# A fused attention and gated-MLP kernel: the first batch by halves of the queries, keys copied whole from the fifth pair on, and a new order

## The chip, the cores and the metric

The kernel runs on one core of one Trainium2 chip. The core has five engines that run side by side, each through its own list in order: TensorE (PE, the matrix engine), VectorE (DVE), ScalarE (ACT), GpSimd (POOL) and SyncE (SP, which here only issues transfers). The metric is the time of one execution on the device in microseconds (us). Lower is better.

## What is computed

Attention over 4 batches x 8 heads, 768 positions of 64, then a gated MLP over 4 batches of 768 rows of 512. Attention sees only 6 of the 24 chunks of 32 keys, chosen by an upper bound of the score per chunk:

```
ub = sum(maximum(q * k_min_of_chunk, q * k_max_of_chunk))     # per query and chunk, causal
mask = (chunk of key is among the 6 largest ub) & (key <= query)
attn = softmax(where(mask, q k^T / 8, -1e9));  x = attn v      # heads side by side: 512
h = gelu(x w_in);  u, v = halves of h (512 each)
v_n = (v - mean) / sqrt(var + 1e-6) * g_ln
v_s = w_sg v_n + b_sg                                          # over the 768 positions
out = x + (u * v_s) w_out
```

## The kernel before

**How the work is laid out.** The heads go in 16 pairs; four pairs make a batch. A pair's q, k and v arrive as rows (L519, L528). PE transposes them in groups of three (L536). DVE reduces the keys to minima and maxima per chunk (L564), ACT or DVE copies keys and queries out of PSUM (L441, L444), and POOL casts the queries (L611). PE computes the bounds (`ub`, L646 for pairs 0 to 3, L693 from pair 4 on, two pairs at once), and DVE turns them into a mask: transposes, the largest eight, a comparison, a transpose back (L656 to L673, L702 to L721). Pairs 0 to 3 add the mask to the scores by extra matmuls (L812) with a table IND. From pair 4 on the mask's rows lie in the same operand as the queries (QA), and INDF beside the keys (KA), so that one matmul does both (L765). For that, KA of each head holds 64 rows of keys and 64 of INDF. ACT takes the exponential (L821 and L771), POOL clears what lies above the diagonal (L828, L776), PE multiplies by v (`pv` off the diagonal L844, `pvd` on it L851), and DVE divides by the sums (`rcp` L859, `xs` L861). PE transposes x (`xtr`, L873) and ACT copies it (`xev`, L441).

When a batch's four pairs are done, the MLP follows: the v half of x w_in with gelu (`hv` L889, `gv` L894), its statistics on DVE (`bns` L899), the inverse deviation on POOL (L905), the normalised v (`vhat`, L917), the u half (`hu` L928, `gu` L934), the product with w_sg (`pt`, L946), and on DVE the gating (L963, which adds b_sg, and L967), then w_out (L979), the sum with x (L988) and the store.

**What sets the order.** The building code creates operations one after another and numbers them. Each names what it reads and writes, from which the waits are worked out. The order in which each engine runs its operations is written out by hand in a table, a list of numbers per engine, with a slot for every PSUM tile. Nothing is reordered at run time: an engine, SP too, that waits holds all that stands behind. PSUM has two score slots of 1024 columns and four general slots of 512. Attention times v uses general slots 2 and 3.

**What the change touches.** `scores` (pairs 0 to 3) cuts its 2688 columns per head into pieces of 512, in the order diagonal blocks first; `head` does a whole head; `xtrans` 768 queries at once; `moe_h` splits batch 0's w_in products into three quarters and one quarter of the inner dimension (HSPL). `kside` copies keys in two halves of 64 partitions for pairs 4 to 7 and in one of 128 from pair KSPR = 8 on, where two transfers then move head 1's keys (`kcp`, L577) and put INDF into head 0's operand (`kin`, L580). For pairs 4 to 7, `mask_rows` puts INDF there by a DVE copy (L735) and a transfer (L738). IND's three further copies and INDF are made on DVE (L403, L408). Transfers of k, q and v have three buffers each, so that a load waits for the transposes of the pair three earlier.

Of the kernel before, what the change touches and what calls it, by code (L numbers as in the profile page):

```python
# [6 lines left out]
ALU = mybir.AluOpType  # L7
# [224 lines left out]
def dve(n, over=70, rate=1.0):  # L232
    o = n / rate / 0.96 + over
    return o, o + 83
# [26 lines left out]
def _build(nc, ctx, q, k, v, w_in, g_ln, w_sg, b_sg, w_out, out):  # L261
# [58 lines left out]
    KSPR = 8  # L320
# [5 lines left out]
    HSPL = 1  # L326
    STACT = 1
    INDV = 1
# [69 lines left out]
    for n, (lo, j) in enumerate(((32, 1), (64, 0), (96, 1))):  # L398
        if INDV == 2:
# [5 lines left out]
        else:  # L405
            P.op("act", lambda d, lo=lo, j=j: d.activation(IND[lo:lo + 32, j, :], IND[0:32, 0, :], ACTF.Copy), act(S),
                 ("init", 10 + n), reads=["IND"], writes=[("IND", n)])
    P.op("dve", lambda d: d.tensor_tensor(INDF[:], IND[:, 0], IND[:, 1], op=ALU.add), dve(S, rate=2), ("init", 13),  # L408
         port=True, reads=["IND"] + [("IND", n) for n in range(3)], writes=["INDF"])
# [42 lines left out]
    xT1n = [("xT", 1, dk) for dk in range(NDK)]  # L452
# [133 lines left out]
    def qside(p):  # L586
        s, w, r = p % NQS, p % NW, p % NR
        for hf in range(2):
# [3 lines left out]
            evac("dve" if p in QDVE else "act", lambda hf=hf: qT[r][:, TG * hf:TG * hf + TG],  # L592
# [150 lines left out]

    def scores_full(p):
        w, es = p % NW, p % 2
        pieces = []
        for kb in range(NT):
            pieces.append((128 * kb, 128, kb, 128 * kb))
        for kb in range(NT - 1):
            pieces.append((EOFF[kb], S - 128 * (kb + 1), kb, 128 * (kb + 1)))  # L750
        for i in range(2):
            for c, c0 in enumerate(range(0, ETOT, 1024)):
# [10 lines left out]
                def sc(e, t=t, mms=mms, i=i):  # L763
# [10 lines left out]
                    writes=[("E", es, i, x) for x in range(2 * c, min(2 * c + 2, len(ECUT)))], ps=[t], table="exp")  # L774
# [3 lines left out]
                 ("aff", p, i), reads=[("E", es, i, 0), ("E", es, i, 1)], writes=[("Ed", es, i)])  # L778

    def scores(p):  # L780
        w, es = p % NW, p % 2
        u, ux = SEL[p]
        pieces = []
        for kb in range(NT):
            pieces.append((128 * kb, 128, kb, 128 * kb))
        for kb in range(NT - 1):
            pieces.append((EOFF[kb], S - 128 * (kb + 1), kb, 128 * (kb + 1)))
        cuts = [(0, LO), (LO, 512)] + ECUT[1:] if p < UNM else ECUT
        for c, (c0, c1) in enumerate(cuts):
# [13 lines left out]
            def sc(e, t=t, mms=mms, masks=masks):  # L803
# [20 lines left out]
                writes=[("E", es, i, c if p >= UNM else ("u", 0)[c] if c < 2 else c - 1) for i in range(2)],  # L824
                ps=[t], table="exp")
        for i in range(2):
            ev = E[es][:, i, 0:S].rearrange("p (j x) -> p j x", x=128)
            P.op("pool", lambda g, ev=ev: g.affine_select(ev, ev, pattern=[[0, NT], [1, 128]], compare_op=ALU.is_ge,  # L828
                                                          fill=0.0, base=0, channel_multiplier=-1), gps(S),
                 ("aff", p, i), reads=[("E", es, i, 0), ("E", es, i, 1), ("E", es, i, "u")], writes=[("Ed", es, i)])  # L830
# [366 lines left out]
```

## Time and profile before

| | us |
|---|---|
| median of 3 runs | 218.07 |
| lowest and highest | 216.73, 219.51 |
| the profiled execution | 217.9 |
| its span, first to last instruction | 216.2 |
| PE busy | 206.0 |
| DVE busy | 184.8 |
| ACT busy | 167.8 |
| POOL busy | 88.8 |

The clock granted to PE was full (0.999). A row of a group reads: line, engine, operation, what it writes from what it reads, shapes, count; then the busy time in us and the mean of one in ns; then the engine's idle time before it and what ended that. A row of the chain of work that ended last reads: start, length, engine, target, line, count. A row of the stretches gives the stretch, its length, then busy time and count for PE, PE's weight loads, DVE, ACT and POOL, PE's clock, the DMA share and GB/s. A row of the transfers gives the size of one and the us from issue to landing.

### The profile page before, as it was taken

What the parts mean: (1) busy time and instruction counts of PE and PEld (TensorE: products, weight loads), DVE (VectorE), ACT (ScalarE), POOL (GpSimd) and SP (SyncE); (2) the same over time, 40 slices, a digit from 0 to 9 for tenths busy, and PEclk for the clock granted to TensorE, in tenths of its full rate; (3) what the DMA queues carried; (4) which work ended last, traced back from release to release, by engine and by line L of the source; (5) the groups of instructions that cost most, each with busy time, mean ns of one, the idle gap of its engine ahead of it and who ended that gap; (6) DMA issues with size and microseconds to landing.
All of it is one profiled execution on the core that took longest, in us unless ns stands there. A gap on an engine that the chain in (4) does not pass through costs nothing.

```text
span 216.2 us, 6033 instructions
## 1 busy us (share of the span) xinstructions
PE 206.0 (95%) x2380; PEld 136.2 (63%) x2380; DVE 184.8 (85%) x534; ACT 167.8 (78%) x258; POOL 88.8 (41%) x119
## 2 busy tenths in 40 slices
PE   7989979899989999998999999999999999999994
PEld 3457757655756577775466776879645668645652
DVE  3999998799979999994999798987798776779894
ACT  3378989987689899999769999999977978774000
POOL 8426696981255476633220655565202331002000
PEclk9999999999999999999999999999999999999999
DMA  7999999993999978988999555533101004002108
GB/s 154 219 219 227 250 256 276 320 278 88 229 237 228 215 198 219 235 223 200 229 183 236 121 132 157 143 124 88 41 0 27 3 0 149 3 0 97 49 3 291
DMA packets 84331, 34.31 MB, mean 159 GB/s; under 512 B 77136, under 2 KB 79440, under 8 KB 84304
## 3 DMA queue, kind: packets, MB, share of 16 engines
q1 hardware_dynamic: 84016, 33.54, 66.0%
q8 instruction: 19, 0.31, 0.7%
q10 hardware_dynamic: 288, 0.39, 0.5%
q14 instruction: 8, 0.07, 0.1%
HBM read 24.77 MB, written 6.29 MB: 144 GB/s over the span
## 4 chain that ended last, share of the span: by engine, by line
PE 75%; DVE 15%; ACT 5%; DMA 2%; issue 1%; SPq 0%; DVEq 0%
PE PSG L946 15%; PE PSC L765 11%; PE PSG L979 10%; PE PSG L928 9%; PE PSG L889 8%; PE PSG L536 7%; PE PSG L844 6%; DVE W L564 5%; PE PSG L693 3%; ACT E L771 3%; PE PSG L851 2%; DVE stats L899 2%; DMA kn<-in_k_dram 2%; PE PSG L873 1%; PE PSC L806 1%
## 5 line engine op out<-in xcount | busy, mean ns | idle before, releaser
L771 ACT ACTIVATE E<-PSC 128x1024 bf16<-128x1024 f32 (+1 forms) x72 | 63.2, 931 | 4.9 <-PE PSC L765 4.5
L564 DVE TENSOR_REDUCE W<-PSG 128x12 f32<-128x384 f32 x64 | 32.7, 547 | 7.0 <-PE PSG L536 6.9
L765 PE MATMUL PSC<-QA,KA 128*128 128x128 bf16 (+2 forms) x336 | 37.6, 246 | 0.0
L946 PE MATMUL PSG<-wsgT,vhat 128*128 128x384 bf16 x192 | 34.7, 326 | 0.7 <-DVE uT L967 0.5
L776 POOL TENSOR_SCALAR_AFFINE_SELECT E<-E 128x768 bf16<-128x768 bf16 x24 | 20.7, 862 | 32.9 <-ACT E L771 32.8
L611 POOL CAST QA<-qT 64x768 bf16<-64x768 f32 (+1 forms) x28 | 24.1, 862 | 15.4 <-ACT qT L441 12.8
L765 PEld LDWEIGHTS PSC<-QA,KA 128*128 128x128 bf16 x336 | 24.1, 98 | 8.8 <-ACT E L771 2.5
L946 PEld LDWEIGHTS PSG<-wsgT,vhat 128*128 128x128 bf16 x192 | 17.9, 98 | 12.0 <-DVE uT L967 1.0
L928 PE MATMUL PSG<-xT,winb 128*128 128x384 bf16 x128 | 24.2, 327 | 0.0
L963 DVE SCALAR_TENSOR_TENSOR PSG<-PSG,glnT,bsgbc 128x384 f32<-128x384 f32 x32 | 19.6, 619 | 5.1 <-PE PSG L946 4.9
L979 PE MATMUL PSG<-woutb,uT 128*128 128x512 bf16 (+1 forms) x100 | 23.7, 371 | 0.0
L934 ACT ACTIVATE uT<-PSG 128x384 bf16<-128x384 f32 x32 | 15.6, 490 | 10.0 <-PE PSG L928 9.6
L821 ACT ACTIVATE E<-PSC 128x1024 bf16<-128x1024 f32 (+3 forms) x26 | 21.5, 872 | 2.2 <-PE PSC L812 1.8
L889 PE MATMUL PSG<-winb,xT 128*128 128x512 bf16 x96 | 22.7, 380 | 0.2 <-ACT xT L441 0.2
L441 ACT ACTIVATE KA<-PSG 128x384 bf16<-128x384 f32 (+1 forms) x38 | 18.5, 497 | 5.5 <-DVE W L564 5.4
L844 PE MATMUL PSG<-vx,E 128*128 128x65 bf16 x480 | 19.7, 194 | 1.1 <-DVE XS L861 0.6
L621 POOL CAST vx<-vn 128x768 bf16<-128x768 f32 x16 | 13.4, 841 | 17.6 <-DMA vn<-in_v_dram 15.5
L844 PEld LDWEIGHTS PSG<-vx,E 128*128 128x128 bf16 x480 | 17.5, 98 | 3.1 <-DVE XS L861 0.7
L861 DVE TENSOR_TENSOR XS<-PSG,rden 128x384 bf16<-128x384 f32 x32 | 17.7, 554 | 0.9
L967 DVE TENSOR_TENSOR uT<-PSG,uT 128x384 bf16<-128x384 f32 x32 | 17.6, 554 | 0.7
L905 POOL TENSOR_TENSOR rstd<-rstd,neghalf 128x6 f32<-128x6 f32 x4 | 5.3, 1329 | 31.2 <-DVE rstd L903 31.2
L899 DVE BATCH_NORM_STATS2 stats<-vgb 128x6 f32<-128x512 f32 x24 | 16.1, 687 | 2.0 <-ACT vgb L894 1.6
(87 smaller groups left out, 353.8 us busy)
## 6 DMA issues: line engine op xcount, KB each, us to landing
kn<-in_k_dram SPq DMA_DIRECT2D x32, 192.0 KB, 4.6
qn<-in_q_dram SPq DMA_DIRECT2D x32, 192.0 KB, 4.4
vn<-in_v_dram SPq DMA_DIRECT2D x32, 192.0 KB, 4.6
out_dram<-osb SPq DMA_DIRECT2D x18, 256.0 KB, 2.3
uT<-in_moe_w_sg_dram SPq DMA_DIRECT2D x4, 384.0 KB, 5.6
vgb<-in_moe_w_in_dram SPq DMA_DIRECT2D x3, 512.0 KB, 6.1
KA<-INDF SPq DMA_DIRECT2D x12, 96.0 KB, 3.6
out_dram<-vgb SPq DMA_DIRECT2D x4, 256.0 KB, 2.2
```

The lines of the kernel that those rows point to most:

```text
L564: P.op("dve", lambda d, m=m, op=op, src=src, h0=h0, h1=h1: d.tensor_reduce(W[w][:, m, 12 * h0:12 * h1].rearrange("p (h c) -> p h c", h=h1 ...
L611: P.op("pool", lambda g, i=i, r0=r0, r1=r1: g.tensor_copy(QA[w][i or 0][r0:r1, :], qT[r][r0:r1, :]), gps(S, 250 if i == 1 else 150), ("qca ...
L765: r = e.matmul(t.ap()[:, o:o + n], KA[w][i][:, 128 * kb:128 * kb + 128], QA[w][i][:, q0:q0 + n], start=True, stop=True)
L771: P.op("act", lambda e, t=t, c0=c0, c1=c1, i=i: e.activation(E[es][:, i, c0:c1], t.ap()[:, 0:c1 - c0], ACTF.Exp, scale=SCALE), act(c1 - c0 ...
L776: P.op("pool", lambda g, ev=ev: g.affine_select(ev, ev, pattern=[[0, NT], [1, 128]], compare_op=ALU.is_ge, fill=0.0, base=0, channel_multi ...
L821: P.op("act", lambda e, t=t, c0=c0, c1=c1, n=n: e.activation(E[es][:, :, c0:c1], t.ap().rearrange("p (i x) -> p i x", i=2)[:, :, 0:n], ACT ...
L844: r = e.matmul(t.ap()[:, 65 * qb:65 * qb + 65], E[es][:, i, a:a + 128], vx[w][:, kb, i, :], start=first, stop=False, skip_group_check=True)
L889: r = e.matmul(t.ap()[:, 0:F], xT[s][:, dk, 128 * qt:128 * qt + 128], winb[:, dk, F:DFF], start=(dk == 0), stop=(dk == NDK - 1), skip_grou ...
L899: P.op("dve", lambda d, qt=qt, st=st: d.bn_stats(stats[st][:], vg[qt]), dve(F, 60), ("bns", b, qt), reads=[("vg", qt)], writes=[("stats", ...
L928: r = e.matmul(t.ap()[:, 0:TG], winb[:, dk, 128 * fb:128 * fb + 128], xT[s][:, dk, TG * tg:TG * tg + TG], start=(dk == 0), stop=(dk == NDK ...
L946: r = e.matmul(t.ap()[:, 0:TG], vhat[s][:, sb, 128 * fb:128 * fb + 128], wsgT[:, sb, TG * tg:TG * tg + TG], start=(sb == 0), stop=(sb == N ...
L979: r = e.matmul(t.ap()[:, 0:n1 - n0], gT[s][:, fb, 128 * qt:128 * qt + 128], woutb[:, fb, n0:n1], start=(fb == 0), stop=(fb == NF - 1))
```

## The change

It does these things:

- Pairs 0 to 3 (Q2 = 4): the columns of the scores are laid out by halves of the queries, 768 columns for queries 0 to 383 and 1920 for the rest, with cuts at 512, 768, 1280, 1792, 2304 and 2688. The diagonal is cleared in two operations a head instead of one, and `head` does each half by itself: two tiles, two `rcp`, two `xs`.
- Batch 0: x^T goes by halves of the queries (eight groups and eight copies for four), and the w_in products depend on one half only. The split of the inner dimension is gone (HSPL = 0), and with it these products use general slots 2 and 3 only, as in batches 1 and 2. The gelus of the two halves are marked as two runs.
- KSPR = 4: the keys of pairs 4 to 7 are copied whole, and `kcp` and `kin` transfers take the place of DVE's copy of INDF.
- IND's three copies become transfers on SP (INDV = 3), and INDF is added on POOL (INDP = 1).
- All order lists, the slots and the filler counts are new. There are 1368 operations for 1338: PE 392 for 386, ACT 248 for 252, DVE 414 for 406, POOL 124 for 115, SP 190 for 179.

Read by the operations' numbers, the new lists say this around batch 0. On PE all pv of pairs 0 to 3 and all x^T groups come before the first w_in product, as they did, and three w_sg transposes instead of two. On ACT the 14 gelus of batch 0 come after the last exp of pair 3 and before the first of pair 4. Between its w_in products PE has ten groups of q and k transposes for pairs 6 to 8 where it had four. On POOL three of the four casts of w_in follow pair 3's last diagonal. On SP the load of b_sg, which stood before pair 4's mask rows (`qd`), stands behind them.

```diff
-    KSPR = 8
+    KSPR = 4
...
-    HSPL = 1
+    HSPL = 0
...
-    INDV = 1
+    INDV = 3
+    INDP = 1
+    Q2 = 4
...
+        if INDV == 3:
+            P.op("sp", lambda e, lo=lo, j=j: e.dma_start(IND[lo:lo + 32, j, :], IND[0:32, 0, :]), dmac(), ("init", 10 + n),
...
+    P.op("pool" if INDP else "dve", lambda d: d.tensor_tensor(INDF[:], IND[:, 0], IND[:, 1], op=ALU.add),
...
+    def pieces_of(p):
+        if p >= Q2:
+            return [(128 * kb, 128, kb, 128 * kb) for kb in range(NT)] + \
+                [(EOFF[kb], S - 128 * (kb + 1), kb, 128 * (kb + 1)) for kb in range(NT - 1)]
+        r, a = [], 0
+        for h in range(2):
+            for kb in range(3 * h, 3 * h + 3):
+                r.append((a, 128, kb, 128 * kb))
+                a += 128
+            for kb in range(3 * h + 2):
+                q0 = max(128 * (kb + 1), TG * h)
+                r.append((a, TG * (h + 1) - q0, kb, q0))
+                a += TG * (h + 1) - q0
+        return r
...
-        cuts = [(0, LO), (LO, 512)] + ECUT[1:] if p < UNM else ECUT
+        cuts = [(0, 512), (512, S), (S, 1280), (1280, 1792), (1792, 2304), (2304, ETOT)] if p < Q2 else ECUT
+        if p < UNM:
+            cuts = [(0, LO), (LO, 512)] + cuts[1:]
...
+        for half in range(2) if p < Q2 else (None,):
+            q0, q1 = (0, NT) if half is None else (3 * half, 3 * half + 3)
+            nq, tg = q1 - q0, () if half is None else (half,)
+            off = [(kb, qb) for kb in range(NT) for qb in range(max(kb + 1, q0), q1)]
+            t = ps_g.tile((2, 3))
...
+        for half in range(2) if b == 0 and Q2 else (None,):
+            j0, j1 = (0, NT) if half is None else (3 * half, 3 * half + 3)
...
+            evac(XEV[b] if isinstance(XEV[b], str) else XEV[b][dk], lambda j0=j0, n=n: xT[b % 2][:, dk, 128 * j0:128 * j0 + n],
...
+        if halves:
+            for h_ in range(2):
+                for qt in range(3 * h_, 3 * h_ + 3):
+                    v_part(qt)
+                for fb in range(NF):
+                    u_part(fb, h_)
```

193 lines of the change are left out of this document (102 added, 91 removed), and 118 rows, old and new, of the table TABLE.

## The prediction

> **What bounds the kernel now.** I read the page's engine totals first, then the chain of work that ended last.
>
> ```profile
> PE 206.0 (95%) x2380; PEld 136.2 (63%) x2380; DVE 184.8 (85%) x534; ACT 167.8 (78%) x258; POOL 88.8 (41%) x119
> ```
>
> TensorE (PE) looks full, but a busy PE isn't a PE at its peak. So I cut the span at five marks taken from the timeline and asked for busy times by stretch: 45.70 is the first matmul of batch 0's w_in products, 59.78 its first w_sg product, 99.37 and 114.38 the same two marks of batch 1, and 88.64 the end of a long run of PE pieces in the chain.
>
> ```profile
> core 0: us, PE busy (x) PEld busy (x) DVE busy (x) ACT busy (x) POOL busy (x), PEclk, DMA share, GB/s
> ...
> 4.69:30.00 25.31, 22.90 (x334) 15.34 (x338) 23.99 (x78) 18.91 (x32) 14.23 (x22) 1.00 1.18 234
> 30.00:45.70 15.70, 14.47 (x315) 10.77 (x305) 13.28 (x39) 14.70 (x23) 12.95 (x16) 1.00 1.04 284
> 45.70:59.78 14.08, 14.08 (x106) 8.81 (x104) 13.75 (x48) 10.55 (x19) 5.00 (x7) 1.00 0.75 185
> 59.78:88.64 28.86, 28.31 (x311) 18.95 (x309) 26.88 (x72) 26.21 (x42) 16.17 (x21) 1.00 0.99 218
> 88.64:99.37 10.73, 9.57 (x180) 7.96 (x173) 8.52 (x36) 10.32 (x16) 5.01 (x6) 1.00 0.89 233
> 99.37:114.38 15.01, 14.74 (x117) 8.56 (x117) 13.00 (x44) 11.57 (x23) 4.58 (x5) 1.00 1.07 205
> 114.38:156.00 41.62, 41.62 (x567) 31.42 (x568) 35.86 (x105) 40.41 (x57) 19.93 (x24) 1.00 0.52 129
> ```
>
> The reader is to see that the limit changes. Up to 30 us it is VectorE (DVE): 23.99 of 25.31. From 30 to 45.7 it is ScalarE (ACT): 14.70 of 15.70. From 45.7 to 59.8 DVE is full again (13.75 of 14.08), and the w_sg products wait for its last operation, vhat. From 88.6 to 99.4 ACT is (10.32 of 10.73). Whether PE is at its peak between, I work out from pieces of the chain, each a run of matmuls with nothing between:
>
> ```profile
> 72.27 1.13 PE PSG L693 x32
> ...
> 74.65 0.44 PE PSC L765 x7
> 75.09 0.86 PE PSG L979 x4
> ...
> 77.58 0.65 PE PSG L536 x6
> 78.24 0.88 PE PSC L765 x11
> ...
> 80.64 0.45 PE PSG L844 x15
> ...
> 199.96 7.80 PE PSG L946 x48
> ```
>
> Between the first w_sg product of batch 0 (59.78) and the first w_in product of batch 1 (99.37), PE's order holds 8 w_sg groups of 0.975 (7.80/8: 7.8), 6 w_out groups of 0.86 (5.2), the scores of eight heads at 1.16 (two chunks of 0.44 and one of 640 columns, 0.28) less two chunks done before (8.4), eight heads of attention times v at 0.63 (21 matmuls at 0.45/15: 5.0), two selection groups of 1.13 (2.3), four x^T groups at 0.33 (by columns, from the scores: 1.3) and 17 transposes of q and k at 0.325 (5.5). That is 35.5 us of 39.6. So 4.1 us are lost there, and most of it where ACT is full. A shorter ACT list there, and a shorter DVE list before 59.78, are what can pay.
>
> **The change part by part.** I numbered the operations as the code creates them, and read the old and new order lists by these numbers. Unit costs, from the groups by line:
>
> ```profile
> L403 DVE COPY IND<-IND 32x768 bf16<-32x768 bf16 x3 | 1.1, 351 | 0.1
> ...
> L408 DVE TENSOR_TENSOR INDF<-IND 128x768 bf16<-128x768 bf16 x1 | 0.5, 547 | 0.0
> ...
> L735 DVE COPY KA<-INDF 64x768 bf16<-64x768 bf16 x4 | 2.6, 656 | 0.1
> ...
> L859 DVE RECIPROCAL rden<-PSG 128x6 f32<-128x6 f32 x32 | 6.1, 191 | 5.1 <-PE PSG L851 4.5
> L861 DVE TENSOR_TENSOR XS<-PSG,rden 128x384 bf16<-128x384 f32 x32 | 17.7, 554 | 0.9
> L988 DVE TENSOR_TENSOR osb<-PSG,XS 128x512 f32<-128x512 f32 x18 | 12.1, 681 | 1.5 <-PE PSG L979 1.4
> L564 DVE TENSOR_REDUCE W<-PSG 128x12 f32<-128x384 f32 x64 | 32.7, 547 | 7.0 <-PE PSG L536 6.9
> L441 ACT ACTIVATE KA<-PSG 128x384 bf16<-128x384 f32 (+1 forms) x38 | 18.5, 497 | 5.5 <-DVE W L564 5.4
> L441 ACT ACTIVATE xT<-PSG 128x768 bf16<-128x768 bf16 x16 | 13.1, 824 | 1.7 <-PE PSG L873 1.6
> L611 POOL CAST QA<-qT 64x768 bf16<-64x768 f32 (+1 forms) x28 | 24.1, 862 | 15.4 <-ACT qT L441 12.8 <-PE PSC L765 1.6
> L602 ACT ACTIVATE rT<-qT 128x576 f32<-128x576 f32 x12 | 8.3, 689 | 0.1
> L894 ACT ACT_TABLE_LOAD x4 | 5.1, 1283 | 0.1
> ```
>
> DVE loses three IND copies (3 x 0.351), INDF (0.547) and the four KA copies of pairs 4 to 7 (4 x 0.656): 4.2 us. The halves give it eight more reciprocals (8 x 0.191) and turn eight multiplications of 384 columns into sixteen of 192. From 384 to 512 columns costs 0.127, so a column is 1 ns, and 192 columns take 0.36: 16 x 0.36 less 8 x 0.554 is 1.3. Together 2.9 us come back; DVE's net is -1.3.
>
> ACT loses eight key evacuations (pairs 4 to 7 whole: 4 per pair become 2), 8 x 0.497 = 4.0 us, and gets eight x^T copies of 384 columns for four of 768: 8 x 0.497 less 4 x 0.824, +0.7. The gelu that now may run in two bursts doesn't in this order: all 14 gelus of batch 0 stand between the last exp of pair 3 and the first of pair 4, with only copies and relus among them. In the old order such copies stand in the same run, and the row shows four table loads for four batches. So I cost this at nothing.
>
> The Trainium skill, page "ScalarE: Activation LUTs", section "Table sets: the hidden batching unit", asks that calls be batched by table set, and says that cheap functions like copy are in every set. A real second run would be against that rule, at two loads; by this order the rule gives no extra load either, and the sum is the same.
>
> PE has the same matmuls, in more groups. POOL gets INDF. No addition of this width is on POOL in the trace: a POOL cast of as many columns takes 0.862, two passes 1.7; either way it runs among POOL's first operations and is first read after pair 4's keys, so I take nothing. The IND copies become three small DMAs (48 KB) behind eight loads. The eight transfers of KA (96 KB each) stand in series between a pair's keys and its scores. The nearest transfers:
>
> ```profile
> KA<-INDF SPq DMA_DIRECT2D x12, 96.0 KB, 3.6
> ...
> QA<-Dt SPq DMA_DIRECT2D x24, 36.0 KB, 1.9
> ...
> bsgbc<-in_moe_b_sg_dram SPq DMA_DIRECT2D x1, 384.0 KB, 6.3
> ```
>
> IND lands within 1.9 to 3.6 us; the masked scores that read it wait for eight reductions (8 x 0.547) and a selection anyway: nothing. KA takes two transfers in turn, 7.2 at 3.6 each. Pair 4's keys are read out before pair 3's last exp, and in the new order the scores that need both transfers come five w_sg groups after the first: hidden. Without that cover each pair would cost up to 7.2.
>
> INDF on POOL has a second price. DVE's subtraction of 24 columns should cost a fraction of an operation of 384 (0.554). Beside a POOL cast it took this:
>
> ```profile
> 27.65 0.82 POOL L437 CAST vhat<-uT 128x768 bf16<-128x768 f32 x1
> 27.73 0.78 DVE L583 TENSOR_TENSOR W<-W 128x24 f32<-128x24 f32 x1
> ```
>
> The Trainium skill, page "SBUF — State Buffer", section "SBUF: two separate sides", says that DVE with two SBUF inputs and GpSimd lock each other out for a whole instruction; the trace agrees. By the rows a meeting costs at most 0.6, and four copies of 0.656 that could meet POOL leave DVE; I take 0.
>
> Now the path. Call T the end of pair 3's last exp (41.1).
>
> ```profile
> 40.68 0.41 ACT L821 ACTIVATE E<-PSC 128x256 bf16<-128x256 f32 x1
> ...
> 45.52 1.00 DVE L702 STREAM_TRANSPOSE U<-PSG 128x288 f32<-128x288 f32 x2
> 45.70 4.26 PE L889 MATMUL PSG<-winb,xT 128*128 128x512 bf16 x19
> ...
> 46.72 1.28 ACT L894 ACT_TABLE_LOAD   x1
> ...
> 56.89 2.82 DVE L917 TENSOR_SCALAR vhat<-vgb,mv,rstd 128x512 bf16<-128x512 f32 x6
> ```
>
> Step 1, T. DVE drops 2.3 us ahead of pair 2's masks (IND, INDF, one KA copy), but the new order puts minima and maxima of pair 4 and three half-heads there, so pair 3's masks come where they came. ACT has as many operations up to T as before. I take -0.5 (bounds -1.5 and +1).
>
> Step 2, to the first w_sg product. After T, PE runs two half-heads (0.63 each with the multiplications hidden behind the next), then x^T halves that wait for ACT's copies, then pair 4's selection: DVE starts its transposes at T+3.8, where it now does at T+4.4. The w_in products wait for the last of POOL's w_in casts, three of which now follow pair 3's diagonal masks, with a query cast among them (three of 1024 columns at 1.1, by the columns of the 0.862 row, and 0.862: 4.2): about T+4.2, against T+4.6. From the transposes on DVE has the 14.2 us of before (45.52 to vhat's end), less one w_sg evacuation moved ahead (0.5), plus six reductions of pairs 6 and 7 moved in (6 x 0.547): 17.0. So the w_sg products start at 40.6 + 3.8 + 17.0 = 61.4, 1.6 later than 59.78. But PE has by then done six more transposes of q and k (6 x 0.325) less 0.16 of scores: 1.8. Net -0.2.
>
> Step 3, to batch 1's w_in products. ACT's list there loses five copies and one relu, 5 x 0.497 + 0.689 = 3.2, and DVE's six reductions are done. PE's work is 34.7 by the same sum (14 transposes, 0.16 more of scores). Of 4.1 us lost I let 2.1 remain: 36.8, so 98.2, against 99.37. The bounds are 0 and 4.1 regained; I take the middle, since PE, now 35 of 37, becomes the limit.
>
> Step 4, batch 1's w_in products: the 15.0 of before, less two transposes, with 0.16 more of scores: 14.5, so 112.7, against 114.38, with 0.5 more work done ahead (a transpose and 0.16). After that the work is the same and PE is full (41.62 of 41.62 in the next stretch), so 1.7 + 0.5 = 2.2 us stay to the end: 217.9 - 2.2 = **215.7**. The profiled execution (217.9) stands 0.2 under the median of the three runs, 218.07, so I make no correction.
>
> Step 5, SP. It is a queue in order, and eleven issues are added.
>
> ```profile
> 45.19 2.15 SPq L433 DMA_DIRECT2D bsgbc<-in_moe_b_sg_dram  x1
> 50.76 1.86 SPq L726 DMA_DIRECT2D QA<-Dt  x3
> ```
>
> The broadcast of b_sg (bsgbc) is issued at 45.19, ahead of pair 4's masks, which held SP until 50.76. In the new order it stands behind them, ten issues later. At 0.62 an issue (1.86/3) that is 56.2 with masks at 50, landing at 62.5 with its 6.3; the first product that adds b_sg comes at 61.4 + 0.975, 62.4. I cost it at 0, since two more w_sg groups fit before PE has no free slot; it has no margin.
>
> **The rivals.** *More is gained.* If T comes 1.5 earlier and the ACT-bound stretch gives all 4.1 back, it is 215.7 - 1.0 - 2.1 = 212.6. For: ACT is full in that stretch, and 3.2 us leave its list. Against: DVE is full in step 2. *Nothing is gained.* The reductions moved ahead of vhat make PE idle, and PE takes ACT's place without regaining: step 3 returns 0.8 instead of 2.0 and T comes 0.5 late instead of early: 215.7 + 1.2 + 1.0 = 217.9, as now. For: 13.75 of 14.08 on DVE. *Slower: b_sg comes late.* Its place is SP behind pair 4's masks. PE has slots for two w_sg groups and then stops; past 64 each microsecond is one on the path. It makes the kernel slower than before from 2.2 later than that, 66.2. [...]
>
> **How the numbers follow.** The forecast has 0.50, more gained 0.19, nothing gained 0.20, slower 0.11. The forecast's own range is 214.2 to 217.0. The range leaves out a part of the first rival (0.07) and the last one's upper half and a little more (0.08): 211.8 to 220.8. About 2% (4.4 us) is what a measurement of this kernel can tell from no change: faster than 213.7 is the first rival and a little of the forecast's edge, 0.21; over 222.4 only the late b_sg with more behind it, 0.09; within 2%, 0.70.
>
> **What would show it.** Step 1: the exp that ends pair 3 near 40.6. Step 2: the first w_sg matmul near 61.4, released by DVE's vhat, with one gelu table load per batch. Step 3: ACT's share in the stretch before batch 1's gelu falls, and the first w_in matmul of batch 1 comes near 98. Step 4: the first w_sg matmul of batch 1 near 112.7. Step 5: no wait of the b_sg product for a DMA. Wrong would be: more than one gelu run per batch, PE waiting for keys of pairs 4 to 7 or for w_out, T later than 42, or a time lost after batch 1, where I see no change of work.

## The result, and the profile after

The changed kernel takes 219.75 us (median of 19 runs, 218.06 to 220.96), the kernel before on the same chip 218.93 (19 runs): ratio 1.0053, 95% interval 1.0030 to 1.0075. The forecast was 215.7: 4.05 us under the measured time, and a gain of 1% where a loss of 0.5% was measured. The stated range, 211.8 to 220.8, holds the time. The direction is wrong. The profiled execution has a span of 217.6, where the kernel before had 216.2.

Two stretches of the changed kernel, one ahead of the end of pair 3's last exp (T), one from the first w_sg product of batch 0 to the first w_in product of batch 1, and the page's totals (columns as in the table of stretches above):

```profile
PE 204.9 (94%) x2397; PEld 137.5 (63%) x2412; DVE 182.4 (84%) x542; ACT 163.9 (75%) x254; POOL 91.7 (42%) x128
```

```profile
30.00:42.67 12.67, 12.21 (x274) 9.82 (x272) 10.89 (x43) 12.64 (x20) 11.17 (x19) 1.00 1.04 291
63.81:101.75 37.94, 35.66 (x472) 26.70 (x477) 34.97 (x107) 32.46 (x49) 20.64 (x26) 1.00 0.98 224
```

And the same second stretch in a second profile of the kernel before, which was taken as an experiment below:

```profile
60.48:100.41 39.93, 37.86 (x483) 26.91 (x481) 35.38 (x108) 36.52 (x57) 21.28 (x27) 1.00 0.92 220
```

The savings in work are real: ACT is 3.9 us shorter over the span (163.9 against 167.8; 3.3 by the forecast's sum), and DVE 2.4 (182.4 against 184.8; 1.3 by the sum). That ACT has 4.1 us less in the second stretch (32.46 against 36.52) is another matter: of the eight key and query copies that are fewer there, one is saved by whole keys, and the new order has moved seven to stages ahead of it (`a_none` below). From 30 us to T ACT has no gap left, 12.64 of 12.67. The marks of the forecast, from the timelines of TensorE and ScalarE of the changed kernel:

```profile
47.68 0.82 PE L948 MATMUL PSG<-xT,winb 128*128 128x384 bf16 x4 [0.20 <-DVE U L708]
...
63.81 2.12 PE L1000 MATMUL PSG<-wsgT,vhat 128*128 128x384 bf16 x12
...
101.75 1.67 PE L929 MATMUL PSG<-winb,xT 128*128 128x512 bf16 x7 [0.78 <-ACT xT L447]
...
115.67 2.11 PE L1000 MATMUL PSG<-wsgT,vhat 128*128 128x384 bf16 x12
```

```profile
40.94 1.73 ACT L841 ACTIVATE E<-PSC 128x1024 bf16<-128x1024 f32 x2
...
48.24 1.28 ACT L954 ACT_TABLE_LOAD   x1
```

Beside the forecast's marks stand those of both profiles of the kernel before. They show how far marks move from one execution to the next: about 1 us by the end.

| mark, us | before | before, second profile | forecast | after |
|---|---|---|---|---|
| T | 41.09 | 41.64 | 40.6 | 42.67 |
| first w_in product, batch 0 | 45.70 | 46.04 | 44.8 | 47.68 |
| first w_sg product, batch 0 | 59.78 | 60.48 | 61.4 | 63.81 |
| first w_in product, batch 1 | 99.37 | 100.41 | 98.2 | 101.75 |
| first w_sg product, batch 1 | 114.38 | 115.47 | 112.7 | 115.67 |
| span | 216.2 | 217.2 | 214.0 | 217.6 |

The start is late from T on. The stage from the first w_sg product to batch 1's first w_in product is shorter (37.94 against 39.59 and 39.93), but the stage ahead of it is longer by more (21.14 from T, against 18.69 and 18.84): from T to batch 1's first w_in product the changed kernel takes 59.1 us, the kernel before 58.3 and 58.8. What follows the last mark is as long as it was (101.9 us, 101.8 before).

The masks of pairs 1, 2 and 3 (last step of each, VectorE's timeline), in the changed kernel and in the second profile of the kernel before:

```profile
19.82 0.48 DVE L679 STREAM_TRANSPOSE Dt<-Dn 128x288 bf16<-128x288 bf16 x1
...
28.54 0.43 DVE L679 STREAM_TRANSPOSE Dt<-Dn 128x288 bf16<-128x288 bf16 x1
...
35.38 0.47 DVE L679 STREAM_TRANSPOSE Dt<-Dn 128x288 bf16<-128x288 bf16 x1
```

```profile
19.77 0.47 DVE L673 STREAM_TRANSPOSE Dt<-Dn 128x288 bf16<-128x288 bf16 x1
...
26.74 0.48 DVE L673 STREAM_TRANSPOSE Dt<-Dn 128x288 bf16<-128x288 bf16 x1
...
33.88 0.48 DVE L673 STREAM_TRANSPOSE Dt<-Dn 128x288 bf16<-128x288 bf16 x1
```

Pair 1's mask comes at the same time; pair 2's comes 1.75 us later (28.97 against 27.22). The first theory was that such late masks starve ScalarE and so make T late. The second theory was that VectorE's whole list ahead of T is the bound, the third that transfers landing late take back any lead, the fourth that T hangs on a chain round several engines.

### The profile page after: what moved, and what is told of

Same layout as the page of the kernel before. It is cut to its first block, busy times and chain, and to the rows that moved or that the text cites. A ratio compares the mean times of both kernels' runs of the same rounds, so it can differ in the third digit from the quotient of the medians.

```text
span 217.6 us, 6124 instructions
## 1 busy us (share of the span) xinstructions
PE 204.9 (94%) x2397; PEld 137.5 (63%) x2412; DVE 182.4 (84%) x542; ACT 163.9 (75%) x254; POOL 91.7 (42%) x128
## 4 chain that ended last, share of the span: by engine, by line
PE 71%; DVE 18%; ACT 5%; DMA 2%; issue 2%; POOL 1%; SPq 0%; DVEq 0%
PE PSG L1000 13%; PE PSC L787 10%; PE PSG L948 8%; PE PSG L929 8%; PE PSG L1033 8%; PE PSG L542 6%; DVE W L570 6%; PE PSG L871 5%; PE PSG L699 3%; PE PSG L905 2%; PE PSG L877 2%; DMA kn<-in_k_dram 2%; DVE W L589 1%; PE PSC L826 1%; DVE vhat L982 1%
## 5 line engine op out<-in xcount | busy, mean ns | idle before, releaser
L798 POOL TENSOR_SCALAR_AFFINE_SELECT E<-E 128x768 bf16<-128x768 bf16 x24 | 21.1, 878 | 31.0 <-ACT E L793 30.7
L841 ACT ACTIVATE E<-PSC 128x1024 bf16<-128x1024 f32 (+4 forms) x26 | 21.3, 865 | 2.1 <-PE PSC L832 2.1
L929 PE MATMUL PSG<-winb,xT 128*128 128x512 bf16 x92 | 21.8, 379 | 1.1 <-ACT xT L447 0.8
L1033 PE MATMUL PSG<-woutb,uT 128*128 128x512 bf16 (+1 forms) x89 | 21.5, 369 | 0.6
L871 PE MATMUL PSG<-vx,E 128*128 128x65 bf16 x480 | 21.1, 194 | 0.9 <-DVE XS L889 0.8
L889 DVE TENSOR_TENSOR XS<-PSG,rden 128x384 bf16<-128x384 f32 (+1 forms) x40 | 18.9, 474 | 1.1
L447 ACT ACTIVATE qT<-PSG 128x384 f32<-128x384 f32 x28 | 13.3, 496 | 8.0 <-PE PSG L542 8.0
L447 ACT ACTIVATE KA<-PSG 128x384 bf16<-128x384 f32 x30 | 15.1, 512 | 4.0 <-DVE W L570 3.8
L934 ACT ACTIVATE vgb<-PSG 128x512 f32<-128x512 f32 x24 | 14.0, 597 | 5.3 <-PE PSG L929 5.3
```

The lines of the kernel that those rows point to most:

```text
L447: P.op("act", lambda e: e.activation(dst(), src(), ACTF.Copy), act(n), tag, reads=reads, writes=writes, ps=ps, shift=shift)
L841: P.op("act", lambda e, t=t, c0=c0, c1=c1, n=n: e.activation(E[es][:, :, c0:c1], t.ap().rearrange("p (i x) -> p i x", i=2)[:, :, 0:n], ACT ...
L871: r = e.matmul(t.ap()[:, 65 * (qb - q0):65 * (qb - q0) + 65], E[es][:, i, at[kb, qb]:at[kb, qb] + 128], vx[w][:, kb, i, :], start=x == 0, ...
L929: r = e.matmul(t.ap()[:, 0:F], xT[s][:, dk, 128 * qt:128 * qt + 128], winb[:, dk, F:DFF], start=(dk == 0), stop=(dk == NDK - 1), skip_grou ...
L1033: r = e.matmul(t.ap()[:, 0:n1 - n0], gT[s][:, fb, 128 * qt:128 * qt + 128], woutb[:, fb, n0:n1], start=(fb == 0), stop=(fb == NF - 1))
```

## Experiments: which part does it

All ratios are to the kernel before on the same chip. First each part was undone alone.

**IND back on VectorE** (`a_ind`).

```diff
-    INDV = 3
-    INDP = 1
+    INDV = 1
+    INDP = 0
```

> The changed kernel with IND's three copies and INDF back on DVE, at the places of the old order; all else as changed. Theory 1 (the new startup order makes the masks of pairs 2 and 3 late, its parts are innocent): DVE gets 1.6 us of work back ahead of pair 2's masks, so the last exp of pair 3 moves later by 0.5 to 1.6 and the time rises by 0.3 to 1.5 over the changed kernel, to about 1.007 to 1.012 of the kernel before. Rival 2 (the three small transfers hold up the loads behind them on SP): the time falls by 0.5 to 1.2, to the kernel before or under it.

Measured 219.61, ratio 1.0047 (1.0015 to 1.0078): as the changed kernel. T came at 42.07, but batch 1's first w_in product at 101.75 again. IND's transfers and INDF on GpSimd are neutral in time, as the prediction had them; neither move expected for this run came.

**Keys of pairs 4 to 7 in halves again** (`a_k8`).

```diff
-    KSPR = 4
+    KSPR = 8
```

> The changed kernel with the keys of pairs 4 to 7 evacuated by halves again (KSPR = 8): eight more ACT copies, four DVE copies of INDF, eight transfers fewer. Theory 1: whole keys are what gives 1 to 2.5 us back between the first w_sg product of batch 0 and that of batch 1, so without them the time rises by 1 to 2.5 over the changed kernel, to 1.010 to 1.017 of the kernel before. Rival (the transfers hold up SP and the loads behind them): the time falls by up to 1.

221.56, ratio 1.0141 (1.0092 to 1.0189), T at 44.47: whole keys gain 1.9 us in this order. They gain it ahead of T, where ScalarE has four more key copies here. From the first w_sg product to batch 1's first w_in product this run takes 37.61 us (66.26 to 103.87), no more than the changed kernel.

**Batch 0 by whole queries again** (`a_q0`), each whole operation where its second half stood.

```diff
-    Q2 = 4
+    Q2 = 0
```

> The changed kernel with pairs 0 to 3 and x^T of batch 0 whole again, each at the place where its second half stood. Rival 3 (the halves' extra DVE operations, 2.9 us, are what costs): the time falls by 1 to 2 under the changed kernel, below the kernel before. Theory 1: the order remains, and the first halves that filled PE are gone: between -0.5 and +1 of the changed kernel.

222.45, ratio 1.0187 (1.0142 to 1.0233), T at 44.35: the halves gain 2.8 us in this order. With whole queries ScalarE stands idle 1.12 us ahead of an exp at 32.00 and 1.27 at 39.00; with halves it has no gap there.

**The new order alone** (`a_none`): all three undone. What is left of the change are the new lists and slots, and HSPL = 0.

```diff
-    KSPR = 4
+    KSPR = 8
-    INDV = 3
-    INDP = 1
-    Q2 = 4
+    INDV = 1
+    INDP = 0
+    Q2 = 0
```

> The new order alone: the changed kernel with keys of the first eight pairs in halves by ScalarE and VectorE as before, batch 0 by whole queries, IND on VectorE; only the order of the lists is the new one. If the parts add up (keys whole were worth 1.9 us and the halves 2.8 us in this order, IND nothing): 4.7 us above the changed kernel, ratio to the kernel before 1.025 to 1.029. If both parts relieve the same stretch of VectorE ahead of T (theory 2): less than the sum, ratio 1.018 to 1.023.

224.36, ratio 1.0270 (1.0231 to 1.0309). The parts add up: 4.7 us above the changed kernel. T came at 45.24, and the first w_sg product at 68.6. So the new order by itself costs 5.9 us, 3.6 of them ahead of T against the second profile, and the parts bring back 4.7. The stage behind the first w_sg product is nearly as short as in the changed kernel, with ScalarE busy 33.61 us instead of 36.52:

```profile
68.60:106.89 38.29, 36.06 (x475) 26.61 (x478) 33.88 (x107) 33.61 (x50) 20.49 (x26) 1.00 0.84 208
```

So it is the order that took the work out of this stage, and it put it ahead: from T to the first w_sg product this run takes 23.4 us.

**Whole keys alone in the old order** (`b_k4`), the transfers put on SP where the changed kernel has them.

```diff
-    KSPR = 8
+    KSPR = 4
```

> The kernel before with one part of the change alone: keys of pairs 4 to 7 whole, with the two transfers a pair put on SP ahead of pair 4's mask rows and, for pairs 6 and 7, behind the loads of pairs 10 and 11. Theory 1: 4 us leave ACT's list and 2.6 DVE's with the startup order unharmed, so 1 to 2 us are gained: 0.991 to 0.996 of the kernel before. Rival (the transfers cost as much as they save): 0.998 or more.

221.39, ratio 1.0116 (1.0060 to 1.0171). T is 40.79 and the first w_in product comes at 44.97, 0.7 earlier than in the first profile of before, but behind it TensorE waits for a whole key's copy and for a head's PSUM tile, and the stage behind the first w_sg product takes 42.3 us (60.32 to 102.61):

```profile
67.12 0.55 PE L542 MATMUL PSG<-identF,kn 128*128 128x128 f32 x3 [1.00 <-ACT KA L447]
...
89.27 0.62 PE L871 MATMUL PSG<-vx,E 128*128 128x65 bf16 x15 [1.26 <-DVE osb L1042]
```

**Halves alone in the old order** (`b_q2`).

```diff
+    Q2 = 4
```

> The kernel before with one part of the change: batch 0's attention, x^T and w_in products by halves of the queries, in the order of before as far as halves allow (their places, and those of a few neighbours ahead of 60 us, chosen anew); keys, IND and the loads as before. If halves gain by themselves what they are worth in the new order (2.8 us): ratio to the kernel before 0.986 to 0.992. Rival (halves only give back what the new order takes from the startup; in the old order the first w_in product waits for the same last head, and VectorE has eight more pairs of reciprocal and product): 0.998 to 1.006.

225.74, ratio 1.0331 (1.0292 to 1.0369). This doesn't price the halves: the places chosen anew also moved the start, and the first mask came at 16.30 instead of 13.5 to 14.1. And all six executions were granted 0.992 of TensorE's clock (0.94 from 30 to 60 us in the profile). Inconclusive. That a part of the change costs time in the other order rests on `b_k4` alone.

**The kernel before once more** (`b_same`), for the spread.

> The kernel before once more, unchanged, for a second profile of it: how far do the marks move from one execution to the next? In its first profile the last exp of pair 3 ended at 41.09 and the first pair's mask was there at 13.49; every profile of the new order, and of the old order with whole keys, has that first mask at 13.6 to 14.6. If the 0.5 us belong to the execution (landing of the first k rows), this profile has the first mask at 13.6 to 14.5 and T later by as much; if they belong to the kernels, 13.4 to 13.6 and T at 41.0 to 41.2.

T at 41.64, the first mask at 14.10, span 217.2. So 0.55 of the 1.58 us by which T seemed late belong to the execution. T is late by 1.0. Counted from the first mask of the same profile T is at 27.6 and 27.5 in the kernel before and at 28.7 in the changed one (42.67 less 13.95), which says nearly the same.

## Experiments: why T is late

**Pair 3's mask early** (`a_d3`), VectorE's list only (`dn` and `dt` are the mask's last two steps; `kmm` are reductions of keys, `wev` copies of w_sg, `rcp` and `xs` the two steps of a half-head):

```diff
-  m8.3 xs.0.0.1 kmm.5.0.0 kmm.5.0.1 wev.1 dn.3 rcp.0.1.1 xs.0.1.1 wev.0 kmm.5.1.1 rcp.1.0.0 xs.1.0.0 dt.3
+  m8.3 dn.3 dt.3 xs.0.0.1 kmm.5.0.0 kmm.5.0.1 wev.1 rcp.0.1.1 xs.0.1.1 wev.0 kmm.5.1.1 rcp.1.0.0 xs.1.0.0
```

> The changed kernel, with one edit in the order of VectorE: the last two steps of pair 3's mask (the difference and its transpose) go up to right behind its MAX8, ahead of pair 0's and pair 1's half heads, the sums of pair 5 and two w_sg copies, so that the mask should be there near 32 us where the changed kernel had it at 35.85. Theory 1 (masks behind other VectorE work starve ScalarE, and that is what made the end T of pair 3's last exp late): T falls from 42.67 to 41.7 to 42.2, ratio to the kernel before 1.000 to 1.003. Theory 2 (VectorE's whole list ahead of T is the bound, and a mask that goes forward only pushes the half heads and sums back): T the same or up to 1 us later, ratio 1.005 to 1.010.

220.26, ratio 1.0089 (1.0051 to 1.0127). The mask is there 4.15 us earlier, at 31.70, and T doesn't follow. VectorE and ScalarE of this run:

```profile
31.22 0.48 DVE L679 STREAM_TRANSPOSE Dt<-Dn 128x288 bf16<-128x288 bf16 x1
```

```profile
41.14 1.73 ACT L841 ACTIVATE E<-PSC 128x1024 bf16<-128x1024 f32 x2
```

T is 42.87. The run has a gain and a loss of its own: pair 2's mask came 0.49 earlier, and ScalarE waits 0.80 at 32.91 for a reduction of pair 5, which the edit pushed back. But in the changed kernel ScalarE has no gap from 28 us to T, so nothing there waits for pair 3's mask; theory 1 falls for this mask.

**Less work on VectorE** (`a_sum`). Pairs 4 and 5 take their chunks' minima and maxima from 8 of 32 rows.

```diff
-                    src(0, 128).rearrange("p h (c x) -> p h c x", x=32), axis=AX.X, op=op),
+                    src(0, 128).rearrange("p h (c x) -> p h c x", x=32)[:, :, :, 0:32 if p not in (4, 5) else 8], axis=AX.X, op=op),
```

> The changed kernel with the block minima and maxima of the keys of pairs 4 and 5 taken over 8 of the 32 rows of a block (so those two pairs select by fewer rows): eight reductions of 0.5 us become some 0.15 us, about 3 us less on VectorE between 25 and 38 us, where it has no idle stretch in the changed kernel. Theory 2 (VectorE's whole list ahead of T is the bound): T falls from 42.67 to 40.5 to 41.7, ratio to the kernel before 0.998 to 1.002. Theory 4 (T hangs on a chain that goes round VectorE, TensorE and ScalarE: pair 2's late queries, its scores, the exps that free the tiles; spare time on VectorE only turns into waits): T at 42.2 to 42.9, ratio 1.003 to 1.007.

220.03, ratio 1.0053 (1.0017 to 1.0088), T at 42.75. The time taken out turns into waits on VectorE:

```profile
26.46 0.48 DVE L662 STREAM_TRANSPOSE U<-PSG 128x288 f32<-128x288 f32 x1 [0.69 <-PE PSG L652]
32.36 0.56 DVE L450 COPY wsgT<-PSG 128x768 bf16<-128x768 bf16 x1 [0.91 <-PE PSG L493]
```

Theory 2 falls: VectorE's total isn't the bound. The first row is pair 2's mask, waiting for its bounds on TensorE. ScalarE still has no gap from 28.0 to T.

**Pair 2's queries loaded earlier** (`a_q2`). In the changed kernel TensorE stops here:

```profile
18.81 0.88 PE L542 MATMUL PSG<-identF,kn 128*128 128x128 f32 x6
20.41 0.52 PE L542 MATMUL PSG<-identF,qn 128*128 128x128 f32 x3 [0.72 <-DVE Dt L679]
```

The row names VectorE, whose pair 1 mask ended at 20.30, but these transposes read head 1's queries of pair 2, a load that SP issued at 14.92 and that took 5.4 us here. One issue was moved on SP (the text on record calls these rows the last quarter):

```diff
-  kn.3.0 kn.3.1 vn.0.0 qn.2.1
+  qn.2.1 kn.3.0 kn.3.1 vn.0.0
```

> The changed kernel with one issue moved on SP: the last quarter of pair 2's q rows goes ahead of pair 3's k rows and of the first v rows, so that it is issued at 12.6 us or so instead of 14.92. Single late load: TensorE's wait at 20.41 (0.72) goes, pair 2's mask comes 0.5 to 0.7 earlier than 28.97, T at 42.0 to 42.3, ratio to the kernel before 1.002 to 1.005. Theory 4 (a chain round several engines): the wait goes and another takes its place; T within 0.3 of 42.67, ratio 1.004 to 1.007.

219.74, ratio 1.0052 (1.0022 to 1.0082). TensorE's wait at 20.41 is gone, so it was the load; pair 2's bounds start at 24.64 instead of 25.05, its mask comes at 28.57 instead of 28.97, and T at 42.25 instead of 42.67: 0.41, 0.40 and 0.42.

What carries this to T is not the mask. ScalarE's last wait ahead of T ends at 27.95 in the changed kernel, a microsecond before that mask, and from there to T it has no gap:

```profile
27.95 0.87 ACT L447 ACTIVATE qT<-PSG 128x384 f32<-128x384 f32 x2 [0.75 <-PE PSG L542]
```

These copies wait for pair 4's queries from TensorE, and those transposes stand in its list right behind the bounds of pairs 2 and 3. So the chain of work that ended last goes:

```profile
25.05 2.38 PE PSG L652 x35
27.95 0.88 ACT qT L447 x2
```

From the end of that wait to T lie 14.7 us in all seven profiles with this list of ScalarE and no later wait (the changed kernel, `a_ind`, `a_ind_kn`, `a_v1`, `a_sum`, `a_q2`, `a_lead`: 14.71 or 14.72). From pair 2's mask to T they have 13.4 to 13.7. In `a_d3` the wait ended at 27.47, and 14.6 and the 0.80 make its T. The kernel before had another limit: its last wait ended later, with less of the list behind it.

```profile
31.06 1.44 ACT L441 ACTIVATE KA<-PSG 64x384 bf16<-64x384 f32 x3 [0.94 <-DVE W L564]
```

That is its second profile; T follows 10.6 later. Up to T ScalarE is busy 30.7 us in the changed kernel and 30.9 in this profile. So T is late by waits alone. Pair 2's bounds start at 25.05 where they started at 23.18, 1.87 later. The late load made 0.4 of it. Where the rest comes from isn't isolated, nor what it costs that pair 3's bounds now stand ahead of pair 4's queries (they were at 30.16): no run moved these alone. One piece is to be seen in the changed kernel, VectorE's subtraction for pair 2, which these bounds wait for, and the one for pair 3:

```profile
24.20 0.80 DVE L589 TENSOR_TENSOR W<-W 128x24 f32<-128x24 f32 x1
...
25.65 0.17 DVE L589 TENSOR_TENSOR W<-W 128x24 f32<-128x24 f32 x1
```

The first takes 0.80 for 24 columns, beside a cast on GpSimd from 23.87 to 24.96, as such a subtraction did before; the second takes 0.17.

Four runs tried other places for many operations at once, chosen with a simple model of the lists. A piece of VectorE's list in `a_place` shows the kind:

```diff
-  dt.0 kmm.2.1.0 kmm.2.1.1 kmm.2.0.1 kmm.2.0.0 rel.1 kev.2.1 qev.3.1 qev.3.0 rel.3 utr.1 m8.1 dn.1 dt.1
+  dt.0 rel.1 kmm.2.0.1 kmm.2.1.0 kmm.2.1.1 qev.3.1 kev.2.1 kev.2.0 kmm.2.0.0 utr.1 m8.1 dn.1 qev.3.0 dt.1
```

> The changed kernel with IND and INDF on VectorE as before and the places of instructions and PSUM tiles ahead of 120 us chosen anew on all five engines (whole keys, halves, one gelu run stay): TensorE keeps 342 of 392 places in sequence, VectorE 331 of 418, ScalarE 207 of 248. Pair 1's bounds and mask go ahead of pair 3's query copies, pair 2's queries and sums come earlier on VectorE, loads of k stand ahead of key copies on SP. Theory 4 (places, not work, make T late): T 1 us or more ahead of 42.67, ratio to the kernel before 0.994 to 1.000. Rival (whatever the places, landings and the full VectorE take a lead back by 102 us): T earlier, ratio 1.002 to 1.006.

> The changed kernel, all its parts as they are, with places over the whole kernel chosen anew but the startup nearly left alone (T expected within 0.4 us of 42.67); loads of k ahead of key copies on SP, evacuations and reductions of the stage from 60 to 100 us in another sequence. If the stage behind the startup holds time that places can give back: first w_in product of batch 1 at 100.8 or earlier, ratio 0.996 to 1.001. Rival (landings pace that stage, and vary from execution to execution): ratio 1.003 to 1.006.

Five of the six executions of `a_place` were granted 0.991 or 0.992 of the clock and aren't compared (median 225.94, no ratio); the sixth, at 0.999, took 221.52; `a_place2` took 227.29, ratio 1.0378 (1.0330 to 1.0426). In both the first mask came late (15.63 and 20.25 against 13.95): what was moved ahead of 14 us spoilt the start. So the next two left that part alone.

> The changed kernel with IND and INDF on VectorE and the places of instructions and PSUM tiles between 14.5 and 120 us chosen anew on all engines; what runs ahead of 14.5 us is left as it is. If places make T late and the stage behind it long: pair 1's to 3's masks earlier, T at 41.6 to 42.2, first w_in product of batch 1 at 100.5 or earlier, ratio to the kernel before 0.996 to 1.001. Rival (what is moved earlier is given back at landings, at PSUM tiles, or at the lock between VectorE and GpSimd): T at 42.3 or later, or earlier without gain at 102 us, ratio 1.003 to 1.010.

> The changed kernel with all its parts, places between 14.5 and 120 us chosen anew for the end of the kernel only: T is to stay where it is (42.4 to 42.9), and the stage from the first w_sg product to the first w_in product of batch 1 is to shrink from 37.94 by 0.9 (loads of k ahead of key copies, other sequences of evacuations). If places hold time there: first w_in product of batch 1 at 100.9 or earlier, ratio 0.998 to 1.002. Rival: the stage stays 37.6 or longer, ratio 1.003 to 1.010.

220.68, ratio 1.0109 (1.0071 to 1.0148), and 221.00, ratio 1.0128 (1.0083 to 1.0174). T was 43.25 and 43.53, and pair 2's mask 29.23 and 30.26. The stage behind the first w_sg product did shrink, to 37.1 and 37.3 from 37.94, but the first w_sg product came 1.3 and 0.9 later. They show no better order. Of theory 4 the chain above is shown: VectorE, TensorE's bounds, ScalarE.

## Experiments: why a lead doesn't last

`a_ind` had T 0.60 earlier than the changed kernel, `a_q2` 0.42; neither ended earlier. A timeline of TensorE for each, in this sequence:

```profile
92.70 0.55 PE L542 MATMUL PSG<-identF,kn 128*128 128x128 f32 x3 [0.84 <-DMA kn<-in_k_dram]
```

```profile
93.51 0.55 PE L542 MATMUL PSG<-identF,kn 128*128 128x128 f32 x3 [1.13 <-DMA kn<-in_k_dram]
```

The same k load is waited for: head 1's rows of pair 10, which SP issues behind pair 8's key copy, a step that itself waits for an evacuation.

**That load ahead of the key copy, with IND on VectorE** (`a_ind_kn`).

```diff
-  kn.10.0 kcp.8 kn.10.1
+  kn.10.0 kn.10.1 kcp.8
```

> The changed kernel with IND and INDF made on VectorE as before (that run had its first w_sg product 0.64 us earlier than the changed kernel, 63.17 against 63.81, yet its first w_in product of batch 1 at the same 101.75, and in it TensorE waits 0.84 us for a k load at 92.70), and one edit more on SP: the second half of pair 10's k load is issued ahead of the key copy of pair 8, which waits for its evacuation. Theory 3 (the lead is lost to this load, which the key copy holds back on SP): the wait at 92.70 goes, the first w_in product of batch 1 comes near 101.1, ratio to the kernel before 1.001 to 1.003. Rival (the lead would be lost anyway, to VectorE or ScalarE in the same stage): wait gone or smaller, but w_in at 101.6 to 101.8, ratio 1.004 to 1.006.

219.36, ratio 1.0050 (1.0021 to 1.0080). The k wait is gone, but neither expected mark came: T was 42.65 (its first mask 0.6 later than the changed kernel's), and batch 1's first w_in product 103.06. In this execution b_sg landed late for VectorE, and w_out later for GpSimd (a wait of 3.28 at 73.34, where the changed kernel has 1.59):

```profile
64.90 0.62 DVE L1017 SCALAR_TENSOR_TENSOR PSG<-PSG,glnT,bsgbc 128x384 f32<-128x384 f32 x1 [0.77 <-DMA bsgbc<-in_moe_b_sg_dram]
```

`a_d3` waits 0.52 at the same place. So b_sg, which the new order issues at 59.65, has no margin.

**A sixth of the v traffic of pairs 4 to 15**, in both kernels (`a_v1`, `b_v1`); the rest of v is left out.

```diff
-                vn[s][:, :, i, :], bass.AP(v.tensor, (2 * p + i) * S * DH,
-                                           [[DH, 128], [128 * DH, NT], [1, DH]])), dmac(),
+                vn[s][:, 0:(NT if p < 4 else 1), i, :], bass.AP(v.tensor, (2 * p + i) * S * DH,
+                                           [[DH, 128], [128 * DH, NT if p < 4 else 1], [1, DH]])), dmac(),
```

> The changed kernel with less to load: of the 24 v loads of pairs 4 to 15 only the first 128 rows of each head are moved (one sixth of 192 KB), the rest of the tile keeps older rows; every instruction stays. The DMA engines are 90 to 99% busy up to about 65 us in both kernels, and three runs of the new order whose first w_sg product came 0.4 to 0.9 us earlier had lost that lead by 102 us, each at another load (a k load, b_sg, w_out). Theory 3, widened (from 45 to 100 us the new order is paced by landings, so that a lead is given back to whichever load is late): with a sixth of the v traffic the first w_in product of batch 1 comes 0.8 us or more earlier than 101.75, ratio to the kernel before 0.995 to 1.001. Rival (VectorE, 27.6 of 28.9 us busy between 59.78 and 88.64, paces it): first w_in product at 101.4 or later, ratio 1.003 to 1.006.

> The same cut of the v loads (pairs 4 to 15, one sixth of each moved) in the kernel before, to set beside the changed kernel with that cut. Theory 3: the old order has slack against its loads (no wait for a DMA of more than 0.2 us was seen on TensorE or VectorE from 45 to 100 us), so nothing much moves: ratio 0.997 to 1.000, and the cut kernel of the new order comes down to it or below. Rival: both unchanged, the pair as far apart as the uncut ones.

`a_v1` 219.21, ratio 1.0033 (1.0010 to 1.0056); `b_v1` 218.65, ratio 0.9991 (0.9962 to 1.0020). The stretch from the first w_sg product to batch 1's first w_in product, in `a_v1`:

```profile
64.27:101.09 36.82, 35.98 (x478) 26.39 (x475) 33.62 (x107) 32.53 (x49) 20.75 (x26) 1.00 0.75 188
```

With the DMA share down from 0.98 to 0.75 the stage takes 36.82 instead of 37.94; in the old order the same cut changes nothing (60.68 to 100.28, 39.6). But the stage ahead took 22.0 us from T instead of 21.1, so from T to batch 1's first w_in product only 0.3 us are left (58.8 against 59.1). In time it is worth 0.2%, inside the two intervals. That part of the stage is paced by landings is possible, and not shown by this.

**Three issues moved on SP** (`a_lead`): pair 2's queries as in `a_q2`, that k load as in `a_ind_kn`, and b_sg ahead of pair 4's mask rows, where SP stood idle.

```diff
-  kn.3.0 kn.3.1 vn.0.0 qn.2.1
+  qn.2.1 kn.3.0 kn.3.1 vn.0.0
...
-  ws.2 qd.4.1
+  ws.2 wb qd.4.1
...
-  kn.10.0 kcp.8 kn.10.1
+  kn.10.0 kn.10.1 kcp.8
```

> The changed kernel with three issues moved on SP and nothing else: the last quarter of pair 2's q rows ahead of pair 3's k rows (T was 42.25 with it), b_sg ahead of pair 4's mask rows, where SP stands idle from 49.8 to 52.7, and pair 10's second k quarter ahead of pair 8's key copy. Theory 3 (a lead is lost at these two landings): no wait for b_sg nor for the k load, first w_in product of batch 1 at 101.3 or earlier, ratio to the kernel before 1.001 to 1.004. Rival (another landing or engine takes it: w_out's, the stores', VectorE): first w_in product at 101.6 or later, ratio 1.004 to 1.007.

218.89 against 218.70, ratio 1.0012 (0.9983 to 1.0041): level with the kernel before. SP's and TensorE's timelines:

```profile
49.85 0.46 SPq L439 DMA_DIRECT2D bsgbc<-in_moe_b_sg_dram  x1
...
85.92 1.22 SPq L525 DMA_DIRECT2D kn<-in_k_dram  x2
```

```profile
91.03 0.55 PE L542 MATMUL PSG<-identF,kn 128*128 128x128 f32 x3 [0.19 <-DMA kn<-in_k_dram]
...
100.41 1.90 PE L929 MATMUL PSG<-winb,xT 128*128 128x512 bf16 x8 [0.57 <-ACT xT L447]
```

b_sg is issued 9.8 us earlier, the wait for k is 0.19, and batch 1's first w_in product comes at 100.41, 1.34 ahead of the changed kernel, from a T that was 0.60 ahead. In this execution the lead gets through, with these landings out of its way. It is the best version of the new order that was run, 0.9 us under the changed kernel by the two ratios, whose intervals just overlap, and not faster than the kernel before.

## Why the prediction was wrong, step by step

The span came 3.6 us longer than forecast (217.6 against 214.0). By the marks: T +2.1, from T to the first w_sg product +0.3, to batch 1's first w_in product +1.1, to its first w_sg product -0.6, behind it +0.6. Of T's 2.1, 0.55 are the execution's (the second profile of before).

- **Step 1 failed.** It said that "pair 3's masks come where they came", that "ACT has as many operations up to T as before", and took -0.5. The count was right: ScalarE is busy 30.7 us up to T, 30.9 before. The wait was not looked at. ScalarE's last wait ahead of T is for pair 4's queries, behind the bounds of pairs 2 and 3 on TensorE, and T comes 14.7 us after it (`a_q2`, `a_lead` and five more profiles); pair 2's bounds started 1.87 later than in the second profile of before. The bound was given as +1 to a T of 41.1, and T came 1.58 later than that, 1.0 later than in the second profile: the choice was wrong, and by the first profile the bound too. That the order lists alone could cost several microseconds ahead of T (`a_none`: 3.6) was not seen; the counts of work per engine, on which the step rested, had all gone down.
- **Step 2 held in size**, once T is given: w_sg products 21.1 us behind T, forecast 20.8. VectorE's list from pair 4's transposes on took 16.7, forecast 17.0, and began 4.5 behind T, forecast 3.8, so two errors partly cancel. The w_in products didn't wait for POOL's w_in casts, which ended at 46.15, but at 47.68 for VectorE's first transpose of pair 4's bounds.
- **Step 3 had the sign and not the size.** The stage shrank from 39.6 (39.9 in the second profile) to 37.94; forecast 36.8. ScalarE's busy time fell by 4.1 between these marks (36.52 to 32.46), forecast 3.2: eight copies, where five and a relu were counted. As step 2 had it, part of what leaves this stage is done in the one ahead; both together were forecast to gain 0.7, and took 0.8 and 0.3 more than in the two profiles of before. TensorE loses 2.3 us of 37.94, forecast 2.1 of 36.8. What the difference of 1.1 is made of stays open: with fewer bytes the stage took 36.82 (`a_v1`), with earlier issues 37.82 from an earlier start (`a_lead`).
- **Step 4**: 13.9, forecast 14.5. But the 0.5 us "more work done ahead" that was to stay to the end didn't: behind the mark 101.9, forecast 101.3.
- **Step 5 held in the changed kernel, without margin, as it said.** b_sg was issued at 59.65 (forecast 56.2), took 4.8 (6.3) and landed at 64.45 (62.5); its reader came at 65.0 (62.4), late for other reasons. Two variants with an earlier reader waited 0.5 and 0.8. The rival built on it named the right place. No run shows b_sg so late that the kernel would reach 220.8, the top of the range: in the changed kernel the issues from pair 4's masks to b_sg took 0.5 to 0.7 us each, one 1.4.
- **At nothing**: IND's transfers and INDF on GpSimd, right (`a_ind`). INDF took 1.63 us there, estimated 1.7. The gelu stayed one run a batch, one table load at 48.24. The lock between VectorE and GpSimd, taken at 0 where the rows bounded a meeting at 0.6, cost about that at 24.20 (0.80 against 0.17), on the chain to T.

## What to carry to other kernels

When the order is new, find for each stage the one operation behind which the limiting engine runs without a gap, and follow that operation's own chain, its loads included, through the new lists. It is the one that the engine's last wait names. Work per engine says how long the full list is, not when it begins. Before counting a lead as won, look at every transfer that lands within a microsecond of its reader further on: a lead is worth only as much as the smallest of those margins. Of the edits tried on the changed kernel, three issues moved on the queue were the only one that brought its time near the kernel before. And profile the kernel before twice: 0.5 to 1 us of the differences between two traces were the execution's.

## Not expected of the hardware

- The start of one program differs by 0.6 us between executions, and not by the loads: the first mask of the kernel before was there at 13.49 in one profile and at 14.10 in the other, and the span differed by 1.0. The first k rows landed within 0.1 us of each other, but TensorE's first six transposes took 0.88 us in the first and 1.54 in the second:

```profile
4.69 0.88 PE L536 MATMUL PSG<-identF,kn 128*128 128x128 f32 x6
```

```profile
4.76 1.54 PE L536 MATMUL PSG<-identF,kn 128*128 128x128 f32 x6
```

- An addition of 768 bf16 columns on GpSimd took three times what VectorE had needed (0.55). The changed kernel's group by line:

```profile
L414 POOL TENSOR_TENSOR INDF<-IND 128x768 bf16<-128x768 bf16 x1 | 1.6, 1633 | 1.4 <-DMA IND<-IND 1.4
```

- A small transfer inside the core saves little against a load. The transfers' rows of the changed kernel:

```profile
kn<-in_k_dram SPq DMA_DIRECT2D x32, 192.0 KB, 4.2
...
KA<-KA SPq DMA_DIRECT2D x12, 96.0 KB, 3.8
...
IND<-IND SPq DMA_DIRECT2D x3, 48.0 KB, 3.0
```

A quarter of the bytes takes 3.0 us to land, where a whole k load takes 4.2 (medians); the mask rows' transfers of 36 KB take 2.6.
